# Head pairing by four, whole-partition loads of w_in, and fewer weight transfers ahead of chunk 2

## The chip, the cores and the metric

The kernel runs on one core of one Trainium2 chip. The metric is device time of one execution in microseconds (us): 718.02 us before the change (median of 3 runs, 718.01 to 718.25). Every run of every kernel in this study was in the fast state; there is no slow run to leave out. All experiments were correct against the reference, and none gives a wrong result on purpose.

The profile's "span" runs from a core's first to its last instruction. The timed number is 1.7 to 2.1 us longer than the span of the same run (in one run of e7, 2.55 us).

## The reference

The model is a retention block (4 batches, 8 heads, 768 steps, head size 64) followed by a feed-forward block with a quick GELU.

```python
gamma = 1.0 - 2.0 ** (-5.0 - np.arange(H))
for t in range(S):
    state = gamma[None, :, None, None] * state + np.einsum('bhd,bhe->bhde', k[:, :, t], v[:, :, t])
    y[:, :, t] = scale * np.einsum('bhd,bhde->bhe', q[:, :, t], state)
x = y.transpose(0, 2, 1, 3).reshape(B * S, H * D)      # (3072, 512)
h = x @ w_in                                           # w_in (512, 2048)
g = h * (1.0 / (1.0 + np.exp(-1.702 * h)))
out = g @ w_out                                        # w_out (2048, 512)
```

The two weights arrive as 64-bit floats, seen as pairs of 32-bit words. The kernel makes 32-bit floats of them itself; below this is called a **narrow**.

## The kernel before

The retention part works on 24 chunks of 128 steps. For a chunk j, `turn(j)` transposes q and k on TensorE (PE) and lets ScalarE copy them out of PSUM, `attend(j)` makes the scores `pa` on PE and multiplies them by the decay mask on VectorE, and `finish(j)` makes `py` (the chunk's output, from the old state and from the masked scores with v), scales it into `X` on VectorE, and updates the state from `pu`. Four chunks make a block of 512 rows, which then passes through the two products of the feed-forward part. The first block is special: there is nothing yet to overlap with, and its weights are still arriving and being narrowed. This is the order of its start:

```python
    act.dma_start(cold, col_decay)
    # ... four small decay rows on ScalarE's queue ...
    load(0)                  # q, k, v of chunk 0
    fetch()                  # one weight piece, 512 KB
    load(1)
    for _ in range(5):
        fetch()
    # ... identity, masks ...
    turn(0)
    for j in range(CB):      # CB = 4 chunks
        attend(j)
        narrow()
        turn(j + 1)          # also asks for q, k of chunk j + 3
        finish(j)            # also asks for v of chunk j + 2
        if j == 0:
            narrow()
        else:
            up0(0, j - 1)    # up-projection: ph <- X, W
```

A head pair shares the 128 partitions, 64 each: heads 2s and 2s+1. To match this, the channels of w_in were permuted, so that one fetch of w_in was two transfers, each to 64 partitions:

```python
    w1v = moe_w_in.bitcast(U32).rearrange("(o c r d) (f two) -> c r d o f two", o=2, c=2, d=D, two=2)
    def fetch():
        i = fetched[0]
        if i < len(SRC):
            x = raw(i).rearrange("p (n two) -> p n two", two=2)
            if i < NFF:                                          # w_in
                for c in range(2):
                    sp.dma_start(x[c * D:(c + 1) * D].rearrange("p (o f) two -> p o f two", o=2), SRC[i][c])
            else:                                                # w_out
                sp.dma_start(x, SRC[i])
            fetched[0] = i + 1
```

The narrow is one ScalarE operation and a chain of six on VectorE. It ends by fetching the next piece. The first two narrows take one piece, the later ones two:

```python
    def narrow():
        # ... lo, hi: the two 32-bit words; m, w: where the result goes ...
        tc.keep_in_program_order(act.activation(m, hi.bitcast(F32), AF.Abs, scale=2.0 ** 16))
        tc.keep_in_program_order(dve.tensor_scalar(m, m, F64_MOST * 2.0 ** 16, F64_LEAST * 2.0 ** 16,
                                                   op0=ALU.min, op1=ALU.max))
        dve.tensor_scalar(mu, mu, 3, None, op0=ALU.logical_shift_left)
        dve.scalar_tensor_tensor(hi, hi, 0x80000000, mu, op0=ALU.bitwise_and, op1=ALU.bitwise_or)
        dve.tensor_scalar(mu, hi, 0xFF800000, None, op0=ALU.bitwise_and)
        dve.scalar_tensor_tensor(lo.bitcast(F32), lo, 2.0 ** -52, m, op0=ALU.mult, op1=ALU.mult)
        # ...
        dve.tensor_add(w, hi, lo)
        for _ in range(n):
            fetch()
```

PE's order is fixed by hand; the order of the other engines is chosen when the kernel is built. "up-projection" below means one `up0`, 16 matmuls of 128x256. One transfer queue (SyncE's) carries q, k, v and all weights, issued in the order of the program.

## Time and profile before

| | before |
|---|---|
| time | 718.02 us |
| span of the profiled run (its time was 719.43) | 717.7 us |
| PE busy | 693.1 us |
| first, second, third up-projection begin | 33.72, 42.87, 51.47 us |

How to read a line of the profile: PE is TensorE, PEld its weight loads, DVE VectorE, ACT ScalarE, POOL GpSimd; SPq is SyncE's transfer queue. L222 is line 222 of that run's kernel. Then comes what is written <- what is read: `pt` are transposes, `pa` scores, `py` a chunk's output, `pu` the state's update, `ph` an up-projection, `kn_in` is k as loaded. A line in order of time begins with start and length in us; a bracket holds the idle time before it and what ended it. The granted clock (PEclk) is TensorE's, 1.0 at full speed.

The prediction below shows the page's busy shares, the stretches and PE's order of time. Two more views of the kernel before say the same from the other side. The first is the table of PE's waits from 0 to 52 us (what waited, on what, us in total, times, longest):

```profile
PE pt L222 <- DMA q_in<-in_q_dram: 14.7, 3, 8.3
PE pt L222 <- DMA kn_in<-in_k_dram: 1.5, 2, 0.9
PE py L256 <- DVE G L242: 1.2, 2, 0.6
```

14.7 us of waiting are for q, of which 8.29 us are for chunk 2's (4.07 are for chunk 0's at the very start and 2.37 for chunk 1's); VectorE's masked scores (G, L242) hold PE for 1.2 us only. The second is the order of time of SyncE's queue (start, us, issue, count):

```profile
10.47 4.39 SPq L155 DMA_DIRECT2D W<-in_moe_w_in_dram  x6
14.91 2.88 SPq L155 DMA_DIRECT2D G<-in_moe_w_in_dram  x4
18.33 0.37 SPq L113 DMA_DIRECT2D q_in<-in_q_dram  x1
```

q of chunk 2 is issued only after these ten half pieces of w_in. That is the wait which the change goes for.

### The profile page before, as it was taken

The numbers are of one execution on the slowest core, as the hardware profiler recorded it, in microseconds if no ns is written. First come the engines' busy times: TensorE is split into PE (matmuls) and PEld (weight loads), VectorE is DVE, ScalarE is ACT, GpSimd is POOL, SyncE is SP. The second block draws the span as 40 slices with busy tenths as digits, with TensorE's granted clock in tenths as the row PEclk, the third lists the DMA queues.
The fourth block names the chain that finished last, engine by engine and source line by source line (L and its number), as shares of the span: only waits on it lengthen the run. The fifth ranks groups of instructions, "written<-read, shape, count | busy, mean of one in ns | idle before, by whom it ended". The sixth has DMA issues, their size and how long they took to land.

```text
span 717.7 us, 10277 instructions
## 1 busy us (share of the span) xinstructions
PE 693.1 (97%) x4096; PEld 572.5 (80%) x4096; DVE 362.6 (51%) x520; ACT 126.8 (18%) x197; POOL 111.2 (15%) x99
## 2 busy tenths in 40 slices
PE   5599999999999999999999999999999999999997
PEld 4478886446888888888888888888888888888886
DVE  2787898995512742444643444463345373244251
ACT  2232223321000000332000332000233000233000
POOL 2221000000275313000233000121200040200030
PEclk9699999999999999999999999999999999999999
DMA  9978733521002324200333300323300230100001
GB/s 197 222 160 169 188 108 132 183 34 18 16 16 62 72 47 100 46 1 10 76 58 86 68 0 6 74 47 87 70 0 1 50 68 9 39 1 0 16 1 44
DMA packets 143055, 46.31 MB, mean 65 GB/s; under 512 B 130208, under 2 KB 136864, under 8 KB 143008
## 3 DMA queue, kind: packets, MB, share of 16 engines
q1 hardware_dynamic: 135760, 39.10, 25.9%
q10 hardware_dynamic: 7248, 6.57, 2.8%
q8 instruction: 32, 0.52, 0.3%
q14 instruction: 15, 0.12, 0.1%
HBM read 39.33 MB, written 6.29 MB: 64 GB/s over the span
## 4 chain that ended last, share of the span: by engine, by line
PE 76%; DVE 10%; SPq 6%; DMA 4%; issue 2%; ACT 1%; ACTq 0%; DVEq 0%
PE pd L408 29%; PE px L357 15%; PE py L357 12%; PE ph L318 8%; SPq L125 5%; PE ph L305 5%; PE py L258 3%; DVE G L347 2%; PE pa L239 2%; PE py L256 2%; DMA kn_in<-in_k_dram 1%; DVE G L348 1%; DVE G L346 1%; PE pu L272 1%; DMA W<-in_moe_w_in_dram 1%
## 5 line engine op out<-in xcount | busy, mean ns | idle before, releaser
L408 PE MATMUL pd<-W,G 128*128 128x256 f32 x1120 | 251.6, 382 | 0.4 <-DVE G L348 0.3
L408 PEld LDWEIGHTS pd<-W,G 128*128 128x128 f32 x1120 | 210.0, 190 | 31.7 <-DVE G L348 1.2
L357 PE MATMUL px<-X,W 128*128 128x256 f32 x512 | 119.0, 379 | 0.0
L357 PEld LDWEIGHTS px<-X,W 128*128 128x128 f32 x512 | 97.3, 190 | 13.2
L357 PE MATMUL py<-X,W 128*128 128x256 f32 x384 | 90.7, 379 | 0.0
L357 PEld LDWEIGHTS py<-X,W 128*128 128x128 f32 x384 | 73.0, 190 | 9.9
L305 PE MATMUL ph<-X,W 128*128 128x256 f32 x256 | 59.3, 386 | 0.0
L318 PE MATMUL ph<-W,W 128*128 128x512 f32 x128 | 55.1, 592 | 0.0
L305 PEld LDWEIGHTS ph<-X,W 128*128 128x128 f32 x256 | 48.0, 192 | 7.1 <-issue 0.2
L230 POOL TENSOR_TENSOR kd<-kn_in,cold 128x512 f32<-128x512 f32 x13 | 13.5, 1042 | 250.6 <-PE pu L272 201.1
L318 PEld LDWEIGHTS ph<-W,W 128*128 128x128 f32 x128 | 24.3, 190 | 30.2 <-issue 29.2
L349 POOL TENSOR_TENSOR G<-G 128x512 f32<-128x512 f32 x20 | 29.0, 1452 | 115.8 <-DVE G L348 114.4
L242 DVE TENSOR_TENSOR at<-pa,mask 128x512 f32<-128x512 f32 x32 | 20.6, 686 | 45.9 <-PE pa L239 45.9
L286 DVE TENSOR_TENSOR G<-G,sg 128x512 f32<-128x512 f32 x48 | 33.1, 689 | 13.7 <-ACT sg L284 13.7
L284 ACT ACTIVATE sg<-G 128x512 f32<-128x512 f32 x48 | 30.3, 630 | 50.8 <-DVE G L367 30.5
L284 ACT ACTIVATE sg<-ph 128x512 f32<-128x512 f32 x32 | 19.1, 597 | 101.7 <-PE ph L305 58.2
L408 PE MATMUL pd<-W,W 128*128 128x256 f32 x160 | 35.6, 380 | 0.4 <-DVE W L348 0.3
L408 PEld LDWEIGHTS pd<-W,W 128*128 128x128 f32 x160 | 30.2, 190 | 5.6 <-DVE W L348 1.2
L262 DVE TENSOR_TENSOR X<-py,rowd 128x512 f32<-128x512 f32 x20 | 13.7, 687 | 36.3 <-PE py L258 36.3
L395 ACT ACTIVATE u<-pd 128x512 f32<-128x512 f32 x6 | 3.6, 597 | 151.4 <-PE pd L408 151.4
L367 DVE TENSOR_TENSOR G<-py,p 128x512 f32<-128x512 f32 x16 | 11.1, 692 | 37.8 <-PE py L357 37.8
L381 DVE TENSOR_TENSOR G<-py,vv 128x512 f32<-128x512 f32 x16 | 11.1, 692 | 25.4 <-ACT vv L378 25.4
(95 smaller groups left out, 641.5 us busy)
## 6 DMA issues: line engine op xcount, KB each, us to landing
v_in<-in_v_dram SPq DMA_DIRECT2D x24, 256.0 KB, 4.6
W<-in_moe_w_in_dram SPq DMA_DIRECT2D x24, 256.0 KB, 6.1
out_dram<-o ACTq DMA_DIRECT2D x24, 256.0 KB, 2.4
kn_in<-in_k_dram SPq DMA_DIRECT2D x21, 256.0 KB, 4.7
W<-in_moe_w_out_dram SPq DMA_DIRECT2D x10, 512.0 KB, 3.7
q_sq<-in_q_dram SPq DMA_DIRECT2D x256, 16.0 KB, 1.8
k_sq<-in_k_dram SPq DMA_DIRECT2D x256, 16.0 KB, 1.7
G<-in_moe_w_out_dram SPq DMA_DIRECT2D x6, 512.0 KB, 3.6
```

Source lines behind the costliest of these rows:

```text
L125: tc.keep_in_program_order(sp.dma_start(t[r0:r0 + C4, hp], src[b, 2 * hp + r0 // D, rows, d0:d0 + C4].rearrange("(s p) d -> p s d", p=C4)))
L239: pe.matmul(p[:, i, hp, :], KT[j][r, hp, :], QT[j][r, hp, :], start=True, stop=True)
L242: dve.tensor_mul(AT[j][:, i], p[:, i], mask[:, i])
L256: pe.matmul(out, old[k, s, :], qt[k, s, :], start=(s < 2), stop=False, skip_group_check=True)
L258: pe.matmul(out, vn[:, 2 * s + r, :], a[:, r, s, :], start=(not c and s < 2), stop=(s >= 2), skip_group_check=True)
L284: act.activation(s, h, AF.Sigmoid, scale=1.702)
L286: dve.tensor_mul(g, h[:, i], s[:, i])
L305: pe.matmul(h[:, ab], w, X[:, 2 * half + c // 2, c % 2, :], start=(ab == 0 and c == 0), stop=(c == 3), skip_group_check=True)
L318: pe.matmul(h, w, X1[:, c // 2:4:2, c % 2, :], start=(c == 0), stop=(c == 3))
L349: pool.tensor_sub(a[1], a[1], a[0])
L357: pe.matmul(acc[:, u, :], W1[:, 2 * d + u, sa, c, :], X[:, sb, c, :], start=(start and u == 0 and c == 0), stop=(stop and c == 1), skip_gr ...
L408: pe.matmul(p0[:, n, :], g1(m, p, sa)[:, n * P:(n + 1) * P], W2[:, sb, p, :], start=(new and p == 0 and n == 0), stop=(last and p == NP - ...
```

## The change

The intent: heads h and h+4 (not 2s and 2s+1) share the partitions, so that y comes out in the natural order of channels, w_in needs no permutation, and each of its pieces is one transfer to all 128 partitions. q and k of the first eight chunks are loaded in two parts each, to place the heads; k of chunk 0 moves to ScalarE's queue. Of the six fetches ahead of chunk 2's q and k, only two stay there; the others come after `turn(0)` and after chunk 0's `turn(1)`. Besides, PE is given idle transposes at the start (`keep_warm`), and the decays are loaded in other pieces.

```diff
-    w1v = moe_w_in.bitcast(U32).rearrange("(o c r d) (f two) -> c r d o f two", o=2, c=2, d=D, two=2)
+    w1v = moe_w_in.bitcast(U32).rearrange("(c p) (f two) -> p c f two", p=P, two=2)
...
-            if i < NFF:
-                for c in range(2):
-                    sp.dma_start(x[c * D:(c + 1) * D].rearrange("p (o f) two -> p o f two", o=2), SRC[i][c])
-            else:
-                sp.dma_start(x, SRC[i])
+            sp.dma_start(x.rearrange("p (c f) two -> p c f two", c=2) if i < NFF else x, SRC[i])
...                                # head index, in py and pu alike
-            pe.matmul(out, vn[:, 2 * s + r, :], a[:, r, s, :], start=(not c and s < 2), stop=(s >= 2),
+            pe.matmul(out, vn[:, HP * r + s, :], a[:, r, s, :], start=(not c and s < 2), stop=(s >= 2),
...                                # q and k of chunks 0 to 7: two loads each
+            if pairs:
+                for i in range(2):
+                    engine.dma_start(t[:, i:H:2, :], src[:, i * HP:(i + 1) * HP, :])
...
     load(0)
+    act.dma_start(cold, col_decay[:, 0:2 * H])
+    # two rowd pieces, then four tiny pieces of "whole", all on ScalarE's queue
     fetch()
     load(1)
-    for _ in range(5):
-        fetch()
+    fetch()
...
-    turn(0)
+    keep_warm(7)
+    turn(0, lambda: keep_warm(3))
+    for _ in range(2):
+        fetch()
     for j in range(CB):
         attend(j)
         narrow()
         turn(j + 1)
+        if j == 0:
+            for _ in range(2):
+                fetch()
         finish(j)
```

More of the change, by code (lines that the diff above doesn't have):

```diff
@@ L96 @@
     rowd = const.tile([P, HP, P], F32, name="rowd")
-    cold = const.tile([P, 2 * H + HP], F32, name="cold")
+    cold = const.tile([P, 2 * H], F32, name="cold")
+    whole = const.tile([P, 2, 2], F32, name="whole")
     ident = const.tile([P, P], F32, name="ident")
@@ L109, in load, with plain @@
         rows = slice(c * P, (c + 1) * P)
-        def plain(name, src, tag, bufs):
-            QKV[name, j] = two.tile([P, H, D], F32, name=name + "_in", tag=tag, bufs=bufs)
-            sp.dma_start(QKV[name, j], src[b, :, rows, :].rearrange("h p d -> p h d"))
+        def plain(name, src, tag, bufs, pairs=False, engine=sp):
+            t = two.tile([P, H, D], F32, name=name + "_in", tag=tag, bufs=bufs)
+            QKV[name, j] = t
+            src = src[b, :, rows, :].rearrange("h p d -> p h d")
+            if pairs:
+                for i in range(2):
+                    engine.dma_start(t[:, i:H:2, :], src[:, i * HP:(i + 1) * HP, :])
+            else:
+                sp.dma_start(t, src)
         if j < 2 * CB:
             if "q" in what:
-                plain("q", q, "q_sq", 2)
-                plain("kn", k, "k_sq", 2)
+                plain("q", q, "q_sq", 2, True)
+                plain("kn", k, "k_sq", 2, True, sp if j else act)
         else:
@@ L126, in load @@
                             t[r0:r0 + C4, hp],
-                            src[b, 2 * hp + r0 // D, rows, d0:d0 + C4].rearrange("(s p) d -> p s d", p=C4)))
+                            src[b, hp + HP * (r0 // D), rows, d0:d0 + C4].rearrange("(s p) d -> p s d", p=C4)))
                 QKV[name, j] = t
@@ L139 @@
             for r in (W2[:, 4], W2[:, 5], G[:, 6:8].rearrange("p a s t -> p a (s t)"))]
-    SRC = [[w1v[c, h, :, :, 2 * p * P:2 * (p + 1) * P] for c in range(2)] for p in range(NP) for h in range(2)] \
+    SRC = [w1v[:, 2 * h:2 * h + 2, 2 * p * P:2 * (p + 1) * P] for p in range(NP) for h in range(2)] \
         + [w2v[:, f] for f in range(NFF)]
@@ L212, in home, with turn @@
         return G[:, 3 + j % 2].rearrange("p s t -> p (s t)").rearrange("p (a b c) -> p a b c", a=2, b=HP)
-    def turn(j):
+    def turn(j, between=lambda: None):
         for name, store in (("q", QT), ("k", KT)):
@@ L223, in turn @@
                 act.activation(t, p, AF.Copy)
+                between()
             else:
@@ L229, in turn @@
             KD[j] = home(j, "kd")
-            pool.tensor_mul(KD[j], QKV.pop(("kn", j)), cold[:, H:2 * H, None].to_broadcast([P, H, D]))
+            x = QKV.pop(("kn", j)).rearrange("p h d -> p (h d)")
+            x = x.rearrange("p (s r d) -> p r s d", s=HP, r=2) if j < 2 * CB else x.rearrange("p (r s d) -> p r s d", r=2, s=HP)
+            pool.tensor_mul(KD[j].rearrange("p (r s) d -> p r s d", r=2), x,
+                            cold[:, H:2 * H].rearrange("p (r s) -> p r s", r=2)[:, :, :, None].to_broadcast([P, 2, HP, D]))
         if j % CB < 2 or j + 2 < 2 * CB:
@@ L271, in finish @@
             for r in range(2):
-                pe.matmul(u[r * D:(r + 1) * D, s, :], kd[:, 2 * s + r, :], vn[:, 2 * s + r, :],
+                pe.matmul(u[r * D:(r + 1) * D, s, :], kd[:, HP * r + s, :], vn[:, HP * r + s, :],
                           start=(s == 0), stop=True, skip_group_check=True)
@@ L276, in finish @@
         else:
-            pool.tensor_mul(new, old, cold[:, 2 * H:, None].to_broadcast([P, HP, D]))
+            pool.tensor_mul(new, old, whole.rearrange("p a b -> p (a b)")[:, :, None].to_broadcast([P, HP, D]))
             dve.tensor_add(new, new, u)
@@ L437, in down, with keep_warm @@
         return todo
-    act.dma_start(cold, col_decay)
-    for c in range(2):
-        for r in range(2):
-            act.dma_start(
-                rowd[c * D:(c + 1) * D, 2 * r:2 * r + 2],
-                bass.AP(tensor=row_decay.tensor, offset=row_decay.offset + (2 * c + r) * P,
-                        ap=[[0, D], [4 * P, 2], [1, P]]))
-    load(0)
+    load(0)
+    act.dma_start(cold, col_decay[:, 0:2 * H])
+    act.dma_start(rowd[0:D], bass.AP(tensor=row_decay.tensor, offset=row_decay.offset, ap=[[0, D], [2 * P, HP], [1, P]]))
+    act.dma_start(rowd[D:P], bass.AP(tensor=row_decay.tensor, offset=row_decay.offset + P, ap=[[0, D], [2 * P, HP], [1, P]]))
+    W = 2 * H + HP
+    for r in range(2):
+        for i in range(2):
+            act.dma_start(whole[r * D:(r + 1) * D, :, i],
+                          bass.AP(tensor=col_decay.tensor, offset=col_decay.offset + i * D * W + 2 * H + 2 * r,
+                                  ap=[[W, D], [1, 2]]))
     fetch()
     load(1)
-    for _ in range(5):
-        fetch()
+    fetch()
     make_identity(nc, ident)
+    idle = ps.tile([P, HP, P], F32, name="idle", tag="x")
+    def keep_warm(n):
+        for _ in range(n):
+            pe.transpose(idle[:, 0, :], ident, ident)
     for i in range(2):
         for hp in range(HP):
-            h = 2 * hp + i
+            h = HP * i + hp
             dve.tensor_copy(mask[:, i, hp, :], cold[:, h:h + 1].to_broadcast([P, P]))
```

## The prediction

> **What bounds the kernel now.** I read the page first: busy shares, then the slices.
>
> ```profile
> PE 693.1 (97%) x4096; PEld 572.5 (80%) x4096; DVE 362.6 (51%) x520; ACT 126.8 (18%) x197; POOL 111.2 (15%) x99
> ...
> PE   5599999999999999999999999999999999999997
> ...
> PEclk9699999999999999999999999999999999999999
> ```
>
> TensorE is busy for 693.1 of 717.7 us. Only 24.6 us are idle, and the first slices (18 us each) hold most of it. The table of busy time by stretch puts numbers on that. Its columns are the stretch, its length, the busy time of PE, PE's weight loads, VectorE, ScalarE and GpSimd, then the granted clock, the DMA share and GB/s.
>
> ```profile
> 20.00:27.00 7.00, 0.00 (x0) 0.00 (x0) 6.35 (x10) 1.14 (x1) 0.00 (x0) 0.59 1.15 222
> 27.00:34.00 7.00, 6.28 (x57) 5.14 (x58) 4.77 (x6) 2.48 (x3) 1.15 (x1) 0.50 1.13 214
> 34.00:51.50 17.50, 16.29 (x177) 13.64 (x177) 12.95 (x18) 5.47 (x8) 5.12 (x4) 0.97 0.74 160
> 51.50:117.00 65.50, 64.62 (x474) 55.00 (x474) 55.56 (x77) 16.98 (x25) 5.75 (x5) 1.00 0.63 155
> 117.00:700.00 583.00, 581.56 (x3251) 478.46 (x3250) 272.85 (x389) 95.11 (x152) 94.29 (x79) 1.00 0.20 44
> ```
>
> From 51.5 to 700 us PE idles 0.9 + 1.4 = 2.3 us. That part is the matmuls' own length, and the change touches none of them. From 20 to 27 us PE does nothing while the DMA share is full, and the clock drops to half until about 35 us. So only the first 51.5 us can move. PE's order of time shows what it waits for; the brackets hold the idle time before a row and what ended it.
>
> ```profile
> 17.43 1.36 PE L239 MATMUL pa<-G 64*128 64x128 f32 x16
> 27.08 1.12 PE L222 MATMUL pt<-ident,q_in 128*128 128x128 f32 x4 [8.29 <-DMA q_in<-in_q_dram]
> ...
> 33.72 4.31 PE L305 MATMUL ph<-X,W 128*128 128x256 f32 x16
> ...
> 42.87 3.72 PE L305 MATMUL ph<-X,W 128*128 128x256 f32 x16
> ```
>
> After chunk 1's scores (17.43) PE waits 8.29 us for q of chunk 2. That transfer was issued at 18.33, behind six weight fetches of 512 KB, all ahead of it in one queue. The chain of waits says the same of its partner, "19.41 9.29 DMA kn_in<-in_k_dram".
>
> [...] Two stretches of the DMA view, the first nearly all w_in (64 partitions a piece), the second w_out (128 partitions):
>
> ```profile
> DMA packets 1198, 2.18 MB, mean 242 GB/s; under 512 B 135, under 2 KB 135, under 8 KB 1198
> ...
> DMA packets 237, 0.91 MB, mean 362 GB/s; under 512 B 16, under 2 KB 16, under 8 KB 237
> ```
>
> The rows differ too (2 KB against 4 KB packets)[...]. q, k and v alone (54 to 56.5 us, 256 B packets) ran at 217 GB/s, and nothing in the change makes those packets longer. [...] Here four transposes take 1.09 us at 4 us and 0.60 us at 39.55, and two 128x256 matmul groups of 16 take 4.31 and 3.72 us, the first begun slow.
>
> **The change, part by part.**
>
> a) Order of transfers. Counted from the start, q and k of chunk 2 were the end of 768 (chunk 0) + 768 (chunk 1) + 6 x 512 + 512 = 5120 KB; now two fetches stand ahead, so 3072 KB. The decay rows (256 KB) come on top of both. v of chunk 2 is last of the same 6400 KB in both: fetches are moved behind, not dropped.
>
> b) w_in's two 64-partition pieces become one of 128. If it runs at w_out's rate of some 380 GB/s, a 512 KB fetch takes 0.524 MB / 380 = 1.4 us instead of 0.524 / 242 = 2.2 us, so 0.8 us less per fetch. Estimates of arrival (start at 2 us, q/k/v and decay rows at 217 GB/s): q, k of chunk 2 at 2 + 2.36/0.217 + 1.05/0.380 = about 15.6 us, [...]against 27.1 and 28.8. v of chunk 2 (2816 KB of q/k/v, 7 fetches, 256 KB of rows) at 2 + 14.5 + 9.7 = 26 us. At the old w_in rate these would be 18 and 32 us.
>
> c) ScalarE's queue gets longer: two k pieces, cold, two rowd, four tiny "whole" pieces, 9 issues instead of 5, ahead of its table load (1.28 us). In the built order the last "whole" waits for a slot that chunk 0's v frees, at about 7 us. So chunk 0's evacuation moves from 5.26 us to about 8.5, and its scores from 7.85 to about 9.9. This is a loss of 2 us at the start, partly hidden, since chunk 1's q arrives only at 12.3 before and about 10 after.
>
> d) keep_warm: 13 extra 128x128 transposes, at 1.09/4 = 0.27 us each, 3.5 us of PE, all in time when PE would wait (0 to 9.9 us). They may bring full clock sooner, which is worth about 1.0 us on chunk 0's scores (2.08 against 1.16) and as much on py.
>
> e) GpSimd, matmul slices and masks: the same counts and sizes with other strides; I count 0. After 117 us nothing changes but addresses.
>
> **Where the next wait is.** With q and k there, VectorE decides. What it has to finish before the third up-projection, in durations of this trace: scores times mask 4 x 1.28, X 4 x 0.69, states 4 x 0.42, two single narrows at 0.43+0.43+0.69+0.42+0.68+0.98 = 3.6, two double ones at about 6.2, two hidden 0.69. Sum 5.1 + 2.8 + 1.7 + 7.2 + 12.4 + 1.4 = 30.6 us.
>
> ```profile
> 25.89 1.23 DVE L190 SCALAR_TENSOR_TENSOR W<-W,W 128x1024 uint32<-128x1024 uint32 x1
> 27.15 0.69 DVE L191 TENSOR_SCALAR W<-W 128x1024 uint32<-128x1024 uint32 x1
> 27.88 1.23 DVE L192 SCALAR_TENSOR_TENSOR W<-W,W 128x1024 f32<-128x1024 uint32 x1
> ```
>
> In the built order VectorE is strictly serial: chunk 1's masked scores stand behind the first narrow, chunk 2's behind the double narrow. I walked that order: chunk 0's scores done 11 to 12, chunk 1's masks at 20.5 to 22.3, chunk 1's X at 23 to 25, first up-projection at 23 to 26 (before 33.72), chunk 2's masks at 32.3 to 33.3, second up-projection at 34.4 to 35.4 (before 42.87), third at 43.5 to 44.5 (before 51.47). Check: about 11 + 30.6, plus 2 for the last py and pu. Gain at the third up-projection 7.0 to 8.0 us, from where both run the same dense stream with the same backlog. **I take 7 us, since the start of ScalarE is the least sure: 718.0 - 7.0 = 711.0 us**, or 1.0% faster.
>
> **Rivals.**
> - DMA stays the bound: w_in keeps 240 GB/s[...]. Then v of chunk 2 lands at 32 to 33 us, just when the masks are done. It would cost 0 to 2 us: 711 to 713.
> - The clock falls back. In my walk PE idles some 4 us ahead of chunk 1's py and 3.4 ahead of chunk 2's[...]. Each fall costs 1 to 3 us, as half speed did at 27 to 34 us. That makes 713 to 715. For it: the same happened before. Against: the gaps are half as long.
> - VectorE less binding than I think, since GpSimd and DMA release things earlier and PE stays warm: the third up-projection at 40 to 41 and 707.5. Against: 30.6 us of its work is hard to fit in less.
> - The gain is eaten later because VectorE, 85% busy from 51.5 to 117 us (55.56 of 65.5), cannot feed a PE that comes earlier. Against: it comes with the same backlog, and the idle time there was 0.9 us.
>
> **Range and chances.** The sum gives 7; both bad rivals together leave 3, the good one gives 11. So 707 to 715 holds 8 in 10. Faster by over 2% needs 14.4 us, hence the third up-projection at 37 us, before VectorE can have done its 30.6 us from its first data: 0.03. Slower by over 2% needs a long new wait or a clock fall that lasts: 0.02. The rest, 0.95.
>
> **What would show it.** q of chunk 2 waited for until 16 to 18 us rather than 27 shows (a). A w_in fetch stretch at 350 GB/s or more shows (b); 240 refutes it. First evacuation at 8 to 9 us shows (c). Waits of PE's py on VectorE's masks of 3 us or more at chunks 1 and 2 show the new bound. From the third up-projection on, the two PE streams should differ by a constant. The prediction fails if PE waits for v or q past 30 us, if ScalarE's queue holds chunk 0 beyond 12 us, or if gaps grow between 51 and 117 us.

## The result

The changed kernel took 712.93 us (median of 4 runs, 712.27 to 715.21), the kernel before 718.13 us beside it (4 runs). The ratio is 0.9926, 95% interval 0.9897 to 0.9955: 0.7% faster, which counts as within 2%. The prediction had 7.0 us of gain; the medians differ by 5.2. Ratios here and below are the mean time of one kernel's fast runs over that of the other's of the same rounds, so not quite the ratio of the medians. The profiled run took 712.85 us, with a span of 710.8.

The page of the changed kernel, with the lines that answer to the prediction's first:

```profile
PE 692.4 (97%) x4109; PEld 572.5 (81%) x4109; DVE 363.7 (51%) x520; ACT 126.6 (18%) x197; POOL 111.5 (16%) x99
...
PE   6799999999999999999999999999999999999997
...
PEclk9899999999999999999999999999999999999999
```

Busy times are the same; PE has 13 more instructions, the idle transposes. Only the first slices differ. The stretches (columns as in the prediction):

```profile
20.00:27.00 7.00, 6.19 (x59) 5.42 (x60) 6.55 (x10) 2.46 (x2) 2.15 (x2) 0.76 1.17 304
27.00:34.00 7.00, 5.23 (x56) 4.13 (x57) 6.86 (x10) 2.75 (x4) 0.00 (x0) 0.89 0.97 227
...
44.40:110.00 65.60, 64.72 (x474) 55.08 (x474) 55.44 (x77) 16.98 (x25) 6.39 (x5) 1.00 0.46 136
110.00:700.00 590.00, 588.56 (x3283) 484.61 (x3282) 273.44 (x390) 95.31 (x153) 94.29 (x79) 1.00 0.20 43
```

From 20 to 27 us PE was idle before; now it is busy for 6.19 of 7 us. From 44.4 to 700 us, PE idles 0.88 + 1.44 = 2.3 us, as much as before from 51.5 to 700: nothing was gained or lost there. PE's waits from 0 to 50 us:

```profile
PE py L262 <- DVE G L248: 5.2, 3, 2.8
PE pt L224 <- DMA q_in<-in_q_dram: 1.8, 1, 1.8
```

The 14.7 us for q have become 1.8 (what is left of the wait for chunk 0's q, part of which idle transposes now fill), and 1.2 us for VectorE's masked scores have become 5.2. In order of time:

```profile
16.72 0.65 PE L224 MATMUL pt<-ident,q_in 128*128 128x128 f32 x4
...
20.81 0.67 PE L262 MATMUL py<-G,state 64*64 64x128 f32 x16 [2.81 <-DVE G L248]
...
23.55 4.73 PE L311 MATMUL ph<-X,W 128*128 128x256 f32 x16
...
32.16 0.91 PE L262 MATMUL py<-G,state 64*64 64x128 f32 x16 [1.77 <-DVE G L248]
...
35.81 3.73 PE L311 MATMUL ph<-X,W 128*128 128x256 f32 x16
...
44.38 7.17 PE L311 MATMUL ph<-X,W 128*128 128x256 f32 x32
```

q of chunk 2 (16.72) has no bracket: PE does not wait for it at all. The waits are ahead of `py` of chunks 1 and 2 (20.81 and 32.16), and both end with VectorE's masks. VectorE's order of time shows why chunk 2's come late:

```profile
29.60 1.22 DVE L198 TENSOR_TENSOR W<-W 128x1024 f32<-128x1024 f32 x1
30.73 1.28 DVE L248 TENSOR_TENSOR G<-pa,mask 128x512 f32<-128x512 f32 x2
```

The scores were done at 29.4 us (28.21 + 1.16), but the last operation of a narrow (L198) still stood ahead of the masks. The third up-projection begins at 44.38 us, 7.1 earlier than before; the span ends 6.9 us earlier. The first up-projection takes 4.73 us instead of some 3.72: the clock was at half speed from 22.2 to 25.6 us (and again from 32.45 to 35.86).

The view of transfers from 16.5 to 19.5 us, nearly all w_in, and ScalarE's first evacuation:

```profile
DMA packets 590, 1.14 MB, mean 381 GB/s; under 512 B 32, under 2 KB 32, under 8 KB 590
```

```profile
8.75 1.09 ACT L225 ACTIVATE G<-pt 128x512 f32<-128x512 f32 x2
```

w_in went from 242 to 381 GB/s with packets of the same size: 1.9 KB in the mean here (1.14 MB / 590), 1.8 KB in the prediction's stretch (2.18 MB / 1198). So short packets are not what made the halves slow. Whether it is the 64 partitions or twice as many transfers, no run separates.

### The profile page after: what moved, and what is told of

The parts are those of the page before. It is cut to its first block, busy times and chain, and to the rows that moved or that the text cites. A ratio compares the mean times of both kernels' runs of the same rounds, so it can differ in the third digit from the quotient of the medians.

```text
span 710.8 us, 10300 instructions
## 1 busy us (share of the span) xinstructions
PE 692.4 (97%) x4109; PEld 572.5 (81%) x4109; DVE 363.7 (51%) x520; ACT 126.6 (18%) x197; POOL 111.5 (16%) x99
## 3 DMA queue, kind: packets, MB, share of 16 engines
q10 hardware_dynamic: 8848, 6.83, 3.1%
## 4 chain that ended last, share of the span: by engine, by line
PE 76%; DVE 12%; SPq 7%; issue 2%; DMA 2%; ACT 1%; DVEq 0%; ACTq 0%
PE pd L414 28%; PE px L363 16%; PE py L363 12%; PE ph L324 8%; SPq L132 6%; PE ph L311 6%; PE py L264 3%; DVE G L353 2%; PE pa L245 2%; PE py L262 2%; DVE G L354 1%; DVE G L248 1%; DVE G L352 1%; PE pu L278 1%; DMA k_sq<-in_k_dram 1%
```

## The experiments

The theory after the result: the start of the first block is a race of several chains, of transfers (q and k of chunk 2, v of chunk 2) and of VectorE (masks behind narrows). The change takes both transfers out of the race, and VectorE's chain now ends last. Rivals: one part of the change does it all, the other being neutral; or the clock, which still falls twice in the first profile, sets the time rather than VectorE.

In the table, "third" is the start of the third up-projection in the profiled run, in us. Span minus "third" is 666.2 to 666.5 us in every profile but those of e1, e5 and e5b (666.9, 667.05 and 666.9), so except there "third" and the span tell the same. Each experiment is an edit of the changed kernel.

| run | time | before beside it | ratio [95%] | third |
|---|---|---|---|---|
| e0 unaltered, again | 713.0 | 718.77 | 0.9928 [0.9915, 0.9940] | 45.65 |
| e1 w_in in halves | 718.04 | 718.77 | 0.9989 [0.9980, 0.9997] | 48.42 |
| e2 six fetches ahead | 716.95 | 718.77 | 0.9976 [0.9966, 0.9987] | 49.09 |
| e1b both undone | 719.57 | 718.77 | 1.0008 [1.0002, 1.0015] | 52.47 |
| e3 no idle transposes | 714.08 | 718.59 | 0.9940 [0.9928, 0.9952] | 46.61 |
| e4 "whole" later | 711.98 | 718.59 | 0.9914 [0.9894, 0.9933] | 42.49 |
| e5 transposes in the gaps | 712.79 | 718.59 | 0.9921 [0.9907, 0.9935] | 45.05 |
| e7 more VectorE work | 716.86 | 718.59 | 0.9970 [0.9959, 0.9982] | 47.23 |
| e5b transposes in the gaps, as meant | 713.69 | 719.24 | 0.9917 [0.9901, 0.9933] | 45.01 |
| e6 sums on GpSimd | 712.08 | 719.24 | 0.9895 [0.9876, 0.9913] | 44.33 |
| e8 masks ahead of narrows | 713.06 | 719.24 | 0.9909 [0.9889, 0.9929] | 44.90 |
| e9 e8 with e6 | 710.19 | 719.24 | 0.9867 [0.9848, 0.9886] | 42.59 |

The three groups (e0 to e2; e3, e4, e5, e7; the rest) ran on three chips, each with its own runs of the kernel before. Across groups I compare ratios. The unaltered kernel ran in the first group only, so every comparison with it from e3 on is one between chips. In e8 and e9 the order of up-projections is another, so "third" is the third that PE makes.

### The changed kernel once more

> The changed kernel itself, unaltered, as the yardstick for the other three on the same chip. The clock of TensorE fell twice in its first profile (22 to 26 and 32 to 36 us), so I expect the third up-projection at 43.5 to 46.5 us, a span of 709.5 to 713.5 us and a ratio to the kernel before of 0.990 to 0.994.

It repeats: 0.9928 against 0.9926. This run is the measure for the others. Its profile shows how much one kernel's start varies: here the clock rose at 16.4 us rather than at 8.6, fell once (23.2 to 26.6 us) rather than twice, and "third" is 45.65, not 44.38. PE's waits for the masks of chunks 1 and 2 are 3.42 and 2.50 us here, against 2.81 and 1.77.

### w_in in two halves, in the new order

```diff
-            sp.dma_start(x.rearrange("p (c f) two -> p c f two", c=2) if i < NFF else x, SRC[i])
+            if i < NFF:
+                xs = x.rearrange("p (c f) two -> p c f two", c=2)
+                for r in (slice(0, D), slice(D, P)):
+                    sp.dma_start(xs[r], SRC[i][r])
+            else:
+                sp.dma_start(x, SRC[i])
```

> The changed kernel, but each w_in fetch is two pieces of 64 partitions again, in the new order of transfers. VectorE theory (after the reordering VectorE's serial order sets the pace): w_in at some 240 GB/s, yet the third up-projection at 44.4 to 46 us and the time within 1.5 us of the changed kernel's. DMA theory (the one wide transfer is what brings the gain): chunk 2's v lands at 32 us or later and PE waits for it; third up-projection at 47 us or later, time 3 us or more above the changed kernel's.

Measured: 0.9989, a gain of 0.11% or 0.8 us instead of 5.2; "third" is 48.42. That is what the DMA theory expected. PE's order of time in this run:

```profile
36.33 2.03 PE L269 MATMUL py<-G,v_in 128*64 128x128 f32 x16 [0.78 <-DMA v_in<-in_v_dram]
...
46.88 1.15 PE L269 MATMUL py<-G,v_in 128*64 128x128 f32 x16 [0.39 <-DMA v_in<-in_v_dram]
...
48.42 3.72 PE L316 MATMUL ph<-X,W 128*128 128x256 f32 x16
```

Up to the first up-projection this run keeps pace (25.44 us against 26.05 in the unaltered run). Then v of chunks 2 and 3 comes late. SyncE's queue issued v of chunk 2 at 28.46 us here and at 21.73 in the changed kernel, and from 4 to 36 us the transfers ran at 196 to 231 GB/s (means of 4 us) without a pause; so v was late because of the bytes ahead of it and beside it, at that rate. The brackets hold 1.2 us, not the whole 2.8 us between the two values of "third". Most of the rest is the clock: it fell from 36.30 to 39.72 us, where it held in the unaltered run's profile, and the second `py`, its `pu` and the second up-projection took 2.03, 1.12 and 3.99 us instead of 1.14, 0.69 and 3.72, together 1.6 us. This is one profile against another; how much of that fall is due to the late v is not shown.

### Six fetches ahead, w_in whole

```diff
     load(1)
-    fetch()
+    for _ in range(5):
+        fetch()
...
     turn(0, lambda: keep_warm(3))
-    for _ in range(2):
-        fetch()
...
-        if j == 0:
-            for _ in range(2):
-                fetch()
```

> The changed kernel with wide w_in transfers but six of them ahead of chunk 2 again. Estimate: q and k of chunk 2 have 2.36 MB at 217 GB/s and 3.15 MB at 380 GB/s ahead, so they land at 21 to 22.5 us instead of 16 to 17. VectorE theory: X of chunk 1 moves from 22.8 to about 26, the third up-projection to 46.5 to 48, time 2 to 3.5 us above the changed kernel's. If the order of transfers is all that counts, third up-projection at 51 and the whole gain is gone; if the wide transfer is all, 44.4 and nothing is lost.

Measured: 0.9976, a gain of 1.7 us; "third" is 49.09, later than the 46.5 to 48 expected. PE's order of time:

```profile
22.58 1.12 PE L224 MATMUL pt<-ident,q_in 128*128 128x128 f32 x4 [5.14 <-DMA q_in<-in_q_dram]
...
49.09 7.17 PE L311 MATMUL ph<-X,W 128*128 128x256 f32 x32
```

q of chunk 2 is waited for again, for 5.14 us, until 22.58 us. With halves and the same order (next run) it is 27.99, so whole transfers bring it 5.4 us earlier; the new order brings the rest, to 16.72 or less.

### Both undone

The edits of the last two together. What stays of the change are the pairing, the split loads of q and k, the longer ScalarE queue and the idle transposes.

> The changed kernel with both parts taken back: six fetches ahead of chunk 2, each of two 64-partition pieces. What is left are the new head pairing, the split q and k loads, the longer ScalarE queue and the warm-up transposes. If these are worth nothing, as I counted, the first transposes of chunk 2 start at 26 to 28 us, the third up-projection at 50 to 52 us, and the ratio to the kernel before is 0.997 to 1.002. If the warm-up is worth something by itself, ratio below 0.996.

Measured: 1.0008, so 0.6 us slower than the kernel before (0.1 to 1.1). q of chunk 2 is waited for until 27.99 us, as before the change:

```profile
27.99 1.08 PE L229 MATMUL pt<-ident,q_in 128*128 128x128 f32 x4 [8.94 <-DMA q_in<-in_q_dram]
```

**What follows from the four.** Against this kernel, the order alone is worth 0.6 + 0.8 = 1.4 us, whole transfers alone 0.6 + 1.7 = 2.3 us, together 0.6 + 5.2 = 5.8 us. The sum of the parts is 3.7; the 2.1 us between are uncertain by some 1.4 (worked out from the four intervals). The parts are worth more together; the traces suggest why, since each alone leaves one of the two waits: the order alone leaves v late (e1), whole transfers alone leave q late (e2). So the rival that one part does it all falls.

### Without the idle transposes

```diff
-    keep_warm(7)
-    turn(0, lambda: keep_warm(3))
+    turn(0)
```

> The changed kernel without its 13 warm-up transposes. In its two profiles the clock rose at 8.6 us in one and at 16.4 us in the other, with the third up-projection at 44.38 and 45.65 us. If the warm-up is worth what I put down (about 1 us on chunk 0's scores and as much on py), the third up-projection comes at 45.5 to 47 us and the time 0.5 to 2 us above the changed kernel's. If the gaps that follow throw the clock away anyhow, there is no difference beyond 0.5 us.

Measured: 0.9940, 0.12% or 0.9 us less gain than the unaltered kernel. The intervals (0.9928 to 0.9952, and 0.9915 to 0.9940) overlap, so the best guess for the worth of the transposes is some 1 us, and it is not shown.

### The tiny decay pieces later, on another queue

The four `whole` transfers move from ScalarE's queue, ahead of its first evacuation, to SyncE's, after `turn(0)`.

```diff
-            act.dma_start(whole[r * D:(r + 1) * D, :, i],       # ahead of the first fetch
+            sp.dma_start(whole[r * D:(r + 1) * D, :, i],        # after turn(0, ...)
```

> The changed kernel, but the four tiny transfers of the state's decay are issued on the other queue after chunk 0's transposes, so that ScalarE is not held by them. ScalarE then reaches its table load at about 4 us and the first evacuation at about 6.1 us instead of 8.75, chunk 0's scores at about 8.2 instead of 9.9 to 10.2. If the start of ScalarE is on the path, the third up-projection is 1 to 2 us earlier (43 to 44). If the next data (q of chunk 1, w_in) set the pace anyhow, it moves by less than 0.5 us.

Measured: 0.9914, 1.0 us more gain than the unaltered kernel; again the intervals overlap. ScalarE's first evacuation came at 6.21 us instead of 8.75, chunk 0's scores at 8.35 instead of 9.89, and "third" at 42.49, the earliest of all runs; but this profile fell on the fastest of its six runs (710.58 us). 2.5 us at ScalarE became about 1 us in the end, if anything: the loss that the prediction put at "2 us, partly hidden".

### Idle transposes in the gaps, twice

```diff
         if j == 0:
             for _ in range(2):
                 fetch()
+        else:
+            keep_warm(14 if j == 1 else 8 if j == 2 else 0)
```

> The changed kernel with 14 and 8 more idle transposes behind the transposes of chunks 2 and 3, where TensorE waits for VectorE's masks, to hold the clock; VectorE's order is the same. Clock theory (the falls at 22 to 26 and 32 to 36 us cost 1 to 3 us each): no fall after the first rise, py, pu and the first up-projection at full speed (1.15, 0.69 and 3.72 us), third up-projection at 42 to 43.5 us, time 1 to 2.5 us below the changed kernel's. VectorE theory alone (PE's speed is hidden behind VectorE): less than 0.7 us.

By a mistake of mine this kernel went out with 16 and 10 transposes instead of the 14 and 8 of the text, and in that build the first operation of a narrow stands ahead of X of chunk 1 on VectorE. The clock did not fall once after 16.1 us, and yet the gain is 0.9921, as without.

> The fill experiment as it was meant: 14 and 8 idle transposes. The run before it went to the chip with 16 and 10 by my mistake, and there the scheduler had put the next narrow's first operation ahead of chunk 1's X, which held TensorE 1.31 us; here VectorE's order is that of the changed kernel. Clock theory: no fall after the first rise, third up-projection at 43 to 44.3 us, time 0.5 to 2 us below the changed kernel's 713.0. VectorE theory alone: within 0.5 us of it.

With the numbers as meant: 0.9917. In the profile the clock held until 34.2 us, "third" is 45.01; in three of the five runs the mean clock is 1.0, and these are no faster (712.89 to 714.42) than the other two (713.42 and 713.69). The best guesses for the worth of holding the clock are 0.5 us (e5) and 0.8 us (e5b) against the unaltered 0.9928; the intervals would allow some 2. So the falls are likely not what keeps the time up: PE works slower during them, but would have waited for VectorE with the time saved.

The lists of runs speak against calling the falls harmless, though. Of the nine runs of the changed kernel the two with the lowest mean clock (0.992 and 0.993) took 715.2 and 715.3 us, the others 712.3 to 714.1. In e4 the two runs at 0.994 or less took 714.1 and 714.8, the four above 710.6 to 712.0; e6 and e8 show the same order, by 1.3 and 1.9 us. A half-speed window of 3.41 us, such as 22.21 to 25.62 us in the changed kernel's first profile, is 0.0024 of the mean clock. Whether the fall makes such a run long, or a longer wait makes the clock fall, is not shown. And e5 and e5b lose 0.5 to 0.7 us after "third", so they are not a clean test. **How much of the time the falls cost stays open.**

### More work for VectorE

The last sum of the two double narrows in the first block is done twice, with no effect on the result.

```diff
         dve.tensor_add(w, hi, lo)
+        if i in (2, 4):
+            tc.keep_in_program_order(dve.tensor_add(w, hi, lo))
```

> The changed kernel with the last VectorE operation of the two double narrows done twice (same result), some 1.2 and 1.5 us of VectorE work more ahead of the masks of chunks 2 and 3, 2.7 in all. VectorE theory: the third up-projection moves by about 2.7 us, to 47 to 48.5, and the time with it. If VectorE has slack there (DMA or PE sets the pace), by less than 1 us.

Measured: 0.9970, where the unaltered kernel has 0.9928. The two added operations took 1.21 and 1.23 us in the profile, together 2.4 (expected: 2.7); the time rose by 0.0042 x 718.6 = 3.0 us, uncertain by 1.2. PE's waits:

```profile
PE py L264 <- DVE G L250: 7.4, 3, 3.6
```

Work added to VectorE comes out at the end, within the interval in full. Part of it may come by way of the clock: these runs' mean clock is 0.989 to 0.997, and the profile shows falls at 11.9, 22.2 and 35.8 us. Work added at PE in the gaps (e5, e5b) did not come out. **VectorE's chain of masks and narrows is the bound of the start now**, with the share of the clock as said open.

### Sums of the narrows on GpSimd

```diff
-        dve.tensor_add(w, hi, lo)
+        (pool if i < 6 else dve).tensor_add(w, hi, lo)
```

> The changed kernel with the last operation of the first four narrows (0.69, 0.69, 1.22 and 1.52 us of VectorE, 4.1 in all) on GpSimd. VectorE theory: the third up-projection comes 2 to 4 us earlier (41 to 43 us), less than 4.1 where GpSimd and VectorE hold each other up, as the operations of 0.42 us did that took 1.3 beside a GpSimd product. If VectorE has slack, or GpSimd's sums come too late for the up-projections, it stays at 44 us or later.

Four sums, together about 4.1 us, leave VectorE in the first block. Measured: 0.9895, 2.4 us more gain than the unaltered kernel (intervals 0.9876 to 0.9913 against 0.9915 to 0.9940, just apart). In plain time it is 712.08 against 713.0 us; the ratio is larger because the kernel before was slower on this chip (719.24 against 718.77). "Third" is 44.33 in the profile, 1.3 us earlier than in the unaltered run and later than the 41 to 43 expected. Where part of the missing 1.7 us went is seen in VectorE's and GpSimd's orders of time:

```profile
20.21 1.50 DVE L192 SCALAR_TENSOR_TENSOR W<-W,W 128x512 uint32<-128x512 uint32 x1
```

```profile
20.12 1.03 POOL L198 TENSOR_TENSOR W<-W 128x512 f32<-128x512 f32 x1
```

L192 takes 0.69 us on its own; beside GpSimd's sum it takes 1.50 and holds up the second mask of chunk 1 behind it. So here the sum saved 0.69 us on VectorE and cost 0.8. A later sum on GpSimd (41.93 to 44.27 us) makes the weights of the third up-projection, which begins at 44.33.

### Masks ahead of the narrows

The narrow is split at its middle, so that the masks of chunks 1 and 2 don't stand behind a whole one, and `up0(0, 2)` goes behind two units of the next half, since its weights come later. This also has the edit of e4. The diff is shortened.

```diff
-        narrow()
+        if j == 0: narrow()
+        elif j == 1: narrow(); rest = narrow(True)      # True: only the first three VectorE operations
+        elif j == 2: rest(); rest = narrow(True)
+        else: rest()
...
-        else:
+        elif j < CB - 1:
             up0(0, j - 1)
...
-    for n, unit in enumerate([(1, p) for p in range(3)] + [...]):
+    for n, unit in enumerate([(1, 0), (1, 1), (0, 2), (1, 2)] + [...]):
```

> A version of my own: the tiny decay transfers later, chunk 1's and 2's masks ahead of the narrows on VectorE (a narrow is split in two halves around them), and two up-projections of the second half, which need no new weights, ahead of the third of the first half. If VectorE's order is what TensorE waits for, the dense stretch begins at 39.5 to 41.5 us instead of 44.4 to 45.7, and the time is 707 to 710 us; it must not lose it again between 45 and 60 us, where the narrows are later than before. If total VectorE work decides and not its order, 42 us and about 711.

Measured: 713.06 us, ratio 0.9909, not clearly more gain than e4 alone (0.9914). Both expectations failed (707 to 710 us if the order decides, about 711 if the total of VectorE's work does). The order moved the wait; chunk 3's masks are now waited for, for 2.28 us, and the clock fell there too (41.6 us). My reading is that the same amount of VectorE work lies ahead of the same point, so that another order of it gains nothing by itself; that is argued, not shown.

### Masks ahead and sums on GpSimd

The edits of e8 and e6 together.

> The version before it with the last operation of the first four narrows on GpSimd as well. If VectorE still sets the pace there, 1 to 2.5 us faster than that version; if TensorE's own chain or the arrival of the data does, within 0.7 us of it.

Measured: 710.19 us (4 runs, 708.89 to 710.92), ratio 0.9867. That is 9 us under the kernel before, and the interval (0.9848 to 0.9886) lies apart from those of the changed kernel and, just, of e8 (from 0.9889); it overlaps that of e6. **This is the best version found; it beats both kernels.** PE's waits in it:

```profile
PE ph L315 <- DVE X L272: 3.0, 2, 2.7
...
PE py L266 <- DVE G L252: 2.2, 2, 1.6
```

`py` waits 2.2 us instead of 5.2. But the first up-projection now waits 2.7 us for X, which on VectorE stands behind a narrow (21.49 us). VectorE is busy for 28.55 us up to the third up-projection, where the changed kernel has 32.84, and is still what PE waits for.

## Why the prediction was right

It named 711.0 us with a range of 707 to 715; the changed kernel took 712.93. Its steps, one by one:

- **Order and rate of transfers (a, b).** q of chunk 2 was put at about 15.6 us; PE used it at 16.72 without waiting. The rate of w_in was taken from w_out's, some 380 GB/s (362 in the stretch shown, 389 from 88.9 to 90.9 us); it is 381. Both are shown; that whole pieces would reach that rate was the author's estimate, and why they do is not shown. That the two need each other is what the experiments add.
- **The first rival's size.** Narrow w_in was to cost "0 to 2 us: 711 to 713". The run with halves took 718.04, by the ratios 4.4 us more than the unaltered kernel. v of chunk 2 was to land at 32 us; it was issued at 28.46 us and held `py` until 36.33. By then 7.5 MB had been moved (summed from the 4 us means), where the estimate counted 6.8 MB up to that v; the queue had issued pieces of w_in behind it from 29.10 us on, and the mean rate was 196 to 231 GB/s, not 242. And the estimate left out the slow clock behind the late v (1.6 us in the profile).
- **ScalarE's queue (c).** First evacuation at about 8.5 us, measured 8.75; scores at 9.9, measured 9.89. Its worth, about 1 us, is in e4 but within its interval.
- **Idle transposes (d).** Full clock for chunk 0's scores (1.16 us instead of 2.08) came in the profiled run, and not in the next (2.08 at 10.22 us): of the twelve profiles with idle transposes, three have it (the changed kernel, e1b, e7). So that part of the first profile is luck. Worth some 0.9 us, within the intervals.
- **GpSimd counted 0 (e).** Its instructions are the same in number, but beside some of them operations of VectorE took longer. In the changed kernel's orders of time of VectorE and GpSimd:

```profile
12.38 1.30 DVE L189 TENSOR_SCALAR W<-W 128x512 f32<-128x512 f32 x1
13.72 0.43 DVE L191 TENSOR_SCALAR W<-W 128x512 uint32<-128x512 uint32 x1
```

```profile
12.36 1.04 POOL L235 TENSOR_TENSOR G<-kn_in,cold 128x512 f32<-128x512 f32 x1 [2.57 <-DMA kn_in<-in_k_dram]
```

  The first operation (L189) takes 0.42 us elsewhere; here it starts 0.02 us after GpSimd's product and takes 1.30. The kernel before has such pairs as well (L196 took 0.98 us at 18.58 us beside GpSimd's L277, and 0.69 at 23.26 with GpSimd idle), so it does not count against the change.
- **The walk along VectorE.** 30.6 us of work from about 11 us on, or 29.5 without X and state of chunk 3, which in the run come after the third up-projection has begun. To the end of chunk 3's masks (11.18 to 42.10) VectorE is busy for 29.45 of 30.9 us; PE's own work from there to 44.38 is the "plus 2". That the sums agree so well is partly luck: single operations took up to 0.9 us more beside GpSimd, and others less than counted. Third up-projection 43.5 to 44.5, measured 44.38; first 23 to 26, measured 23.55; second 34.4 to 35.4, measured 35.81. In the second profile of the same kernel (e0) they are 26.05, 36.80 and 45.65, outside by 0.05 to 1.4 us. That VectorE bounds the start is shown by e7 (2.4 us of work, 3.0 us of time) and by e6 and e9 in the other direction.
- **The sign of the new bound was set too high.** Waits of `py` for the masks of "3 us or more at chunks 1 and 2" were to show it (the walk had some 4 and 3.4). Measured are 2.81 and 1.77, in e0 3.42 and 2.50: the same waits for the same reason, but shorter.
- **The constant stream after it.** Shown: the idle time from there to 700 us is 2.3 us in both, and span less "third" the same within 0.2 us.
- **The clock falls, as a rival.** The falls came, at the two gaps that the walk named. Their price ("1 to 3 us" each) is not settled: holding the clock gained 0.5 and 0.8 us (e5, e5b; up to some 2 by the intervals), while runs of one kernel with a lower mean clock are longer by 1.3 to 3 us.
- **The term that was mis-sized is the last line of the sum, "718.0 - 7.0".** The 7 us come from the profile of before, whose own run took 719.43 us, while 718.0 is the median. Between the two profiled runs the span fell by 6.9 us and the time outside the span grew by 0.3 (719.43 - 717.7 = 1.73 before, 712.85 - 710.8 = 2.05 after), which gives 712.8. So 1.4 of the 1.9 us of error are a starting point that was not the median run's. Most of the rest is the time outside the span, whose growth I can't explain. This divides the error between two single runs; it does not test the cause. Against the repeat's profile (e0) "third" is only 5.8 us earlier, close to the 5.2 of the medians, so it is partly luck that the first pair of profiles shows the 7 us forecast.

What makes single runs of one kernel differ by up to 3 us (717.55 to 720.65 for the kernel before, 712.85 to 715.30 for the changed one, on the first chip) stays open. The clock goes with it, as the lists of runs show (715.2 and 715.3 us at mean clocks of 0.992 and 0.993, 712.3 to 714.1 above that); but e5's runs with a granted clock of 1.0 still differ by 1.5 us.

## What to carry to other kernels

Where several chains race to the same point, undoing one part of a change measures that part given the others; only the run with neither part shows what they do together. When a wait for a transfer is taken away, add up the work of the engine that is busy meanwhile: here VectorE's 30.6 us told the end to within 1 us in one profile and 2 us in the next, and the gain of 14.7 us of waits was never to be had. A gain read from a profile belongs to the run that was profiled: where runs of one kernel differ by as much as 3 us, look at more than one profile before subtracting it from the median.

## What the traces show of transfers, clock and VectorE

- A stretch of nearly all w_in in halves ran at 242 GB/s (14 to 23 us, kernel before), one in whole pieces at 381 GB/s (16.5 to 19.5 us, changed kernel), with packets of 1.8 and 1.9 KB in the mean. No run here separates the 64 partitions from the number of transfers.
- The clock fell after stretches in which PE was partly busy. In the changed kernel it fell at 22.21 us, rose at 25.62, fell at 32.45 and rose at 35.86; the kernel before was at half clock from 21.32 to 34.98 us. These times lie 3.41, 6.83, 3.41 and 13.66 us apart, that is 1, 2, 1 and 4 times some 3.41, so the traces are read here in windows of that length. The changed kernel's stretches (clock in the third column from the end):

```profile
11.97:15.38 3.41, 2.17 (x36) 1.89 (x36) 3.34 (x5) 1.29 (x3) 1.04 (x1) 1.00 1.20 305
...
18.80:22.21 3.41, 1.40 (x30) 1.26 (x32) 3.34 (x7) 0.45 (x1) 0.54 (x1) 1.00 1.21 302
22.21:25.62 3.41, 3.41 (x28) 2.93 (x24) 3.03 (x6) 2.01 (x2) 1.76 (x2) 0.50 1.08 338
```

  After 1.40 us busy of 3.41 the next window is at half clock, after 2.17 it is not (the window after that, from 15.38, is at 1.00). Of the 17 windows at full clock that I read in five profiles (the changed kernel, e0, e5b, e7, e9), those with PE busy for 0.59 to 1.67 us were followed by half clock, and those with 1.75 us or more by full clock, with one exception at 1.62 (e9, from 20.53 us) that held. The kernel before adds a fall at 21.32 us after 0.88 us busy. The clock rose after windows with 3.04 (e7), 3.09 (the changed kernel), 3.41 (e0) and 3.42 us (the kernel before) and not after 2.13 and 2.77 (e0) nor 0, 1.07 and 2.77 (the kernel before). These were read off, not set by an experiment.
- In the changed kernel the clock rose at 8.56 us after nothing but transposes (3.09 us busy in the window before): four of them took 1.08 us at 5.03 us, 0.66 at 10.98 and 0.65 at 16.72. Chunk 0's scores, next after such transposes, took 1.16 us in e7 (at 10.34 us) and e1b (at 10.68) as well, and 2.08 in e0 (at 10.22).
- Operations of VectorE took longer beside some of GpSimd's: one of 0.42 us (L189) took 1.30 us beside GpSimd's product, and in e6 one of 0.69 (L191, at 42.56 us) took 2.27 beside GpSimd's sum. The prediction counted nothing for this.
